# Weight conversions of a mixed attention and MLP kernel: low parts made by TensorE in place of GpSimd, and copies moved to ScalarE

## The chip, the cores and the metric

The kernel runs on one core of a Trainium2 chip. The metric is the device time of one execution in microseconds, as the median of several runs. The engines are named as the profile names them: PE (TensorE matmul), PEld (its weight loads), DVE (VectorE), ACT (ScalarE), POOL (GpSimd) and SP (SyncE, which issues most DMAs).

## The reference

Three parts follow one another, for 4 batches, 768 tokens and 384 channels (8 heads of 48).

```python
# 1: delta-rule attention, per head, k normalized
for t in range(S):
    y[:, :, t] = q_t @ state
    state = state + beta_t * outer(k_t, v_t - state.T @ k_t)
# 2: Fourier mixing and MLP
u = x + real(fft(fft(x, axis=1), axis=2))
x = u + relu(layernorm(u) @ w_ch1) @ w_ch2          # 384 -> 1536 -> 384
# 3: token mixing
theta = x @ w_theta
u = x + w_tok_r @ (x * cos(theta)) + w_tok_i @ (x * sin(theta))
out = u + relu(u @ w_ch)
```

The weights `w_ch1`, `w_ch2`, `w_theta`, `w_tok_r`, `w_tok_i` and `w_ch` are multiplied in two parts each: a high one in the rounded format fp32r and a low one that holds the rest, with three matmuls for one product (`mm3`). They arrive as 64-bit floats.

## The kernel before

The work is written as one Python program whose instructions a scheduler of the framework orders on each engine, by the order of the program and a simulated timeline. Each engine then runs its own list in order. `tc.issue_after(ins)` puts what is traced inside it behind `ins` on that instruction's engine.

**Attention.** Tokens are taken in 48 scans of one batch and 64 tokens each (8 heads, as 4 pairs). Two scans make a chunk step d (24 of them), four chunk steps a wave w (6). For each wave `gram` loads keys (`kt`) and forms products of keys with keys and queries, which ACT copies to `KQ` (L220) and POOL completes with copies of a diagonal block (L223). `solve` inverts 128 triangular 32x32 systems on DVE: a transpose (L228), a few small instructions with a square root on ACT (L240), then 60 dependent multiplications and additions in a loop (L258, L261). `solved` transposes the result. `chunks(d)` makes from it the operands `YU` of two scans: copies by DVE (L309, L315), matmuls, copies by ACT. `load(d)` fetches queries and keys, `scan(g)` runs the recurrence: matmuls on PE with copies by ACT (L340 and others) between them. The generator `attention_steps` writes these steps out in order, with `SOLVES` and `GRAMS` saying at which chunk step a later wave is solved or formed. `attend(n)` advances it by n yields.

**Weight conversion.** `Split.steps` takes one 128x384 block of a 64-bit weight at a time: SP loads it (`raw`), ACT takes the absolute value of the upper words (L110), DVE assembles the 32-bit float and the rest in six instructions (L111 to L116, on the tiles `a` and `g` that the profile calls `w_0ag`, `w_384ag` and so on by the block's first column), and POOL makes the high part (L120), the difference (L121) and the low part (L122). `w1` and `w2` have 24 blocks together. Twenty are written between the attention steps of batch 0, behind the end of solve 0 on DVE, the others before the first MLP matmul.

**Fourier and MLP.** After the 12 scans of a batch `fourier_inputs` forms sums on DVE and POOL (L395), `fourier_1` and `prepare_1` multiply by constants, normalize (L530 and after) and `prepare_2` transposes. Twelve MLP blocks q (three a batch, 256 tokens each) follow, each with twelve steps f of `ffn_up` (9 matmuls into `ph`, L72 to L74) and `ffn_down` (6 into `pc`, L595 to L598). The preparation of block q+1 is written at f = 0, 4 and 11 of block q (`LEAD`). After each step the attention of the next batches advances by `attend(PACE)`, later the conversion of the token-mixing weights.

**Token mixing.** Phases (`pth`) and products (`ty`, `tc`) follow at the end.

Four PSUM buffers with the tags `g` (three) and `mw` (one) serve nearly all of this until the last part.

Of the kernel before, what the change touches and what calls it, by code (L numbers as in the profile page):

```python
# [33 lines left out]
F64_LEAST = 2.0 ** -15  # L34
F64_MOST = float(np.array([0x47EFFE00], np.uint32).view(np.float32)[0])
# [6 lines left out]
SOLVES = (2, 6, 7, 13, 15)  # L42
GRAMS = (1, 6, 9, 13)
CONV_AT = 0
CONV_PRE = 9
# [7 lines left out]
AHEAD = {3: (), 4: (5,), 5: (6, 7)}  # L53
FIXD = ()
SUBD = 0
# [5 lines left out]
CONV_0 = 1  # L61
FDVE = 2
EVERY = 1
PACE = 2
# [12 lines left out]
class Split:  # L77
# [15 lines left out]
    def steps(self, stage, act=False):  # L93

        nc, step = self.nc, self.STEP
        for c, s in self.todo:
# [40 lines left out]
class Front:  # L137
# [19 lines left out]
    def open_attention(self, ctx):  # L157
# [13 lines left out]
        self.Y3 = [win.tile([P, 2, 8, D], F32, name=f"Y3{i}") for i in range(NY3)]  # L171
        self.beta = self.sml.tile([P, NW, 32], F32, name="beta")
# [28 lines left out]
    def gram(self, w, c0=0, c1=2 * C):  # L201

        nc, FE, TK, B2 = self.nc, self.FE, self.TK, self.B2
        if c0 == 0:
            self.KQ[w] = self.sol.tile([P, NI, 2 * C], F32, tag="KQ", name=f"KQ{w}", bufs=2)
# [3 lines left out]
        for d in range(4 * w, 4 * w + 4):  # L209
            for h in range(0, 8, step):  # L210
                n = slice(8 * (d % 4) + h, 8 * (d % 4) + h + step)
                kt = self.sol.tile([P, step, 8 * C // step], F32, tag="kt", name=f"kt{d}_{h}_{c0}", bufs=NKT)
                for par in range(2):
                    nc.sync.dma_start(kt[FE[par]], src[par, d, :, h:h + step])
                sm = self.mw([P, step, c1 - c0], f"sm{d}_{h}_{c0}")
                for i in range(step):
                    for par in range(2):
                        k = kt[FE[par], i, :]
                        self.mm(sm[TK[par], i, :], k[:, 0:C], k[:, c0:c1])
                nc.scalar.activation(kq[:, n, c0:c1], sm, AF.Copy)  # L220
                if c0 == 0:
                    for par in range(2):
                        (nc.vector if w in FIXD else nc.gpsimd).tensor_copy(kq[B2[par], n, 0:32], kq[B2[par], n, 32:64])  # L223

    def solve(self, w):
        nc, sol, sml = self.nc, self.sol, self.sml
        T = sol.tile([P, 32, 32], F32, tag="T", name=f"T{w}")
        nc.vector.transpose(T.rearrange("p j i -> p j i"), self.KQ[w][:, :, 0:32].rearrange("p n j -> p j n"))  # L228
        diag = T.rearrange("p i j -> p (i j)")[:, 0:1024:33]

        def small(nm, bufs=1):
            return sml.tile([P, 32], F32, tag=nm, name=f"{nm}_{w}", bufs=bufs)

        s0, rc, nr, g, ng = (small(nm) for nm in ("s0", "rc", "nr", "g", "ng"))
        nT = small("nT", 2)
        dg = small("dg")
        nc.vector.tensor_copy(dg, diag)
        nc.gpsimd.affine_select(out=T, in_=T, compare_op=ALU.is_gt, fill=0.0, base=0,
                                pattern=[[1, 32], [-1, 32]], channel_multiplier=0)
# [12 lines left out]
        nc.vector.tensor_tensor(T, T, ng.unsqueeze(2).to_broadcast([P, 32, 32]), ALU.mult)  # L252
        nc.vector.memset(diag, 1.0)
        tmp = sml.tile([P, 256], F32, tag="tmp", name=f"tmp{w}")
        for j in range(1, 31):
            n = 31 - j
# [772 lines left out]
```

## Time and profile before

| | us |
|---|---|
| time, median of 3 runs (lowest to highest) | 1001.59 (1001.2 to 1005.55) |
| profiled execution, span from first to last instruction | 1217.0 |
| PE busy in the span | 1126.0 (93%) |
| DVE busy | 682.7 (56%) |
| ACT busy | 394.8 (32%) |
| POOL busy | 387.5 (32%) |
| mean granted TensorE clock in the profiled execution | 0.666 |

The profiled execution is a single one. Its span is longer than the time of the three runs, and no other time of this execution is recorded. Busy times are unions: matmuls that overlap are counted once. The granted clock is a share of 2.4 GHz.

### The profile page before, as it was taken

How to read it: one execution, taken by the hardware profiler on the slowest of the kernel's cores; microseconds unless marked ns; L12 is line 12 of the kernel's file. 1: busy time of each engine (PE TensorE's matmuls, PEld its weight loads, DVE VectorE, ACT ScalarE, POOL GpSimd, SP SyncE). 2: the span in 40 equal slices, each digit the busy share in tenths (PEclk: the TensorE clock that was granted, in tenths of full speed). 3: DMA queues.
4: the chain of work that ended last, by engine and by line, in shares of the span. 5: the costliest groups of instructions: out<-in, count | busy, mean ns of one | idle time of the engine just before them, and what ended most of it. 6: DMA issues, size and time to landing. Idle time of an engine off the chain costs nothing.

```text
span 1217.0 us, 23437 instructions
## 1 busy us (share of the span) xinstructions
PE 1126.0 (93%) x9312; PEld 957.3 (79%) x9312; DVE 682.7 (56%) x1574; ACT 394.8 (32%) x982; POOL 387.5 (32%) x504
## 2 busy tenths in 40 slices
PE   5675664999999999999999999999999999999998
PEld 4564553778788888788888898888988888888887
DVE  5999999645666632576212464744579732450401
ACT  2243343423332343244352121212545411460300
POOL 5257764341131113024120242430235421350210
PEclk9995555666666666666666666666666666666666
DMA  6223431221030021012030021311132201110000
GB/s 190 70 87 94 121 110 50 79 72 60 29 110 21 28 86 59 27 40 68 27 106 14 26 78 40 91 40 32 47 104 65 85 14 35 38 40 20 20 13 26
DMA packets 42206, 71.87 MB, mean 59 GB/s; under 512 B 6833, under 2 KB 27057, under 8 KB 42097
## 3 DMA queue, kind: packets, MB, share of 16 engines
q1 hardware_dynamic: 41328, 68.02, 18.7%
q0 software_dynamic: 768, 2.36, 0.7%
q8 instruction: 73, 1.20, 0.4%
q14 instruction: 37, 0.30, 0.1%
HBM read 56.20 MB, written 14.16 MB: 58 GB/s over the span
## 4 chain that ended last, share of the span: by engine, by line
PE 83%; DVE 13%; issue 1%; DMA 1%; ACT 1%; POOL 0%; SPq 0%; ACTq 0%; DVEq 0%; POOLq 0%
PE pc L595 6%; PE ph L72 6%; PE ph L74 6%; PE ph L73 6%; PE pc L598 6%; PE pc L596 6%; PE ty L73 6%; PE ty L72 6%; PE ty L74 6%; PE sm L199 3%; PE pm L530 3%; DVE tmp L258 3%; DVE T L261 3%; PE py L199 2%; PE pg L457 2%; PE pu L199 2%
## 5 line engine op out<-in xcount | busy, mean ns | idle before, releaser
L586 DVE SCALAR_TENSOR_TENSOR hl<-ph,hh 128x256 fp32r<-128x256 f32 x144 | 60.1, 421 | 196.6 <-ACT hh L585 164.1
L72 PE MATMUL ph<-uh,w1h 128*128 128x256 f32 x432 | 151.9, 355 | 0.0
L74 PE MATMUL ph<-uh,w1l 128*128 128x256 f32 x432 | 148.5, 345 | 0.0
L73 PE MATMUL ph<-ul,w1h 128*128 128x256 f32 x432 | 148.2, 344 | 0.0
L595 PE MATMUL pc<-w2h,hh 128*128 128x384 f32 x288 | 127.6, 443 | 0.0
L585 ACT ACTIVATE hh<-ph 128x256 fp32r<-128x256 f32 x144 | 54.5, 383 | 208.6 <-PE ph L74 183.0
L596 PE MATMUL pc<-w2l,hh 128*128 128x384 f32 x288 | 121.4, 422 | 0.0
L199 PE MATMUL sm<-kt 48*64 48x128 f32 (+1 forms) x896 | 87.5, 354 | 30.7 <-DMA kt<-in_kq_dram 17.3
L73 PEld LDWEIGHTS ph<-ul,w1h 128*128 128x128 f32 x432 | 100.7, 233 | 6.6 <-issue 2.2
L72 PEld LDWEIGHTS ph<-uh,w1h 128*128 128x128 f32 x432 | 97.4, 226 | 8.3 <-issue 2.5
L74 PEld LDWEIGHTS ph<-uh,w1l 128*128 128x128 f32 x432 | 101.0, 234 | 2.3 <-issue 0.8
L199 PEld LDWEIGHTS sm<-kt 48*64 48x64 f32 x896 | 67.5, 186 | 43.7 <-ACT KQ L220 12.5
L598 PE MATMUL pc<-w2h,hl 128*128 128x384 f32 x288 | 98.2, 425 | 0.0
L261 DVE TENSOR_TENSOR T<-T,tmp 128x30 f32<-128x30 f32 (+9 forms) x180 | 73.1, 406 | 4.2
L258 DVE TENSOR_TENSOR tmp<-T 128x30 f32<-128x30 f32 (+9 forms) x180 | 72.9, 405 | 4.3
L284 POOL TENSOR_SCALAR_AFFINE_SELECT YQ<-KQ 64x512 f32<-64x512 f32 x48 | 33.1, 690 | 131.5 <-PE py L199 122.8
L199 PE MATMUL py<-X,YQ 112*64 112x48 f32 (+1 forms) x768 | 54.4, 259 | 22.3 <-ACT X L340 22.1
L595 PEld LDWEIGHTS pc<-w2h,hh 128*128 128x128 f32 x288 | 63.3, 220 | 8.4 <-issue 4.0
L596 PEld LDWEIGHTS pc<-w2l,hh 128*128 128x128 f32 x288 | 63.2, 220 | 7.2 <-issue 1.7
L199 PE MATMUL pu<-X,YU 128*64 128x48 f32 (+1 forms) x768 | 46.2, 262 | 23.6 <-ACT X L352 11.7
L199 PEld LDWEIGHTS py<-X,YQ 112*64 112x64 f32 (+1 forms) x768 | 45.3, 184 | 28.7 <-ACT X L340 23.9
L199 PEld LDWEIGHTS pu<-X,YU 128*64 128x64 f32 (+1 forms) x768 | 38.7, 181 | 33.9 <-ACT X L352 12.2
(282 smaller groups left out, 2524.6 us busy)
## 6 DMA issues: line engine op xcount, KB each, us to landing
kt<-in_kq_dram SPq DMA_DIRECT2D x96, 96.0 KB, 2.2
w_0raw<-in_w_dram SPq DMA_DIRECT2D x15, 384.0 KB, 3.4
YQ<-in_qt_dram SPq DMA_DIRECT2D x48, 96.0 KB, 2.4
Y<-in_kn_dram SPq DMA_DIRECT2D x48, 96.0 KB, 2.4
X<-in_v_dram SPq DMA_DIRECT2D x48, 96.0 KB, 2.5
ysc<-y SPq DMA_DIRECT2D x24, 192.0 KB, 2.1
x2scr<-u SPq DMA_DIRECT2D x12, 384.0 KB, 2.8
xt<-x2scr SPq DMA_DIRECT2D x24, 192.0 KB, 2.4
```

The source lines that it names most:

```text
L72: nc.tensor.matmul(out, lh, rh, start=start, stop=False)
L73: nc.tensor.matmul(out, lh, rl, start=False, stop=False)
L74: nc.tensor.matmul(out, ll, rh, start=False, stop=stop)
L199: self.nc.tensor.matmul(o, l, r, start=True, stop=True, skip_group_check=True)
L258: nc.vector.tensor_tensor(pr, T[:, j + 1:, j:j + 1].to_broadcast([P, n, j]), T[:, j, 0:j].unsqueeze(1).to_broadcast([P, n, j]), ALU.mult)
L261: nc.vector.tensor_tensor(T[:, j + 1:, 0:j], T[:, j + 1:, 0:j], pr, ALU.add)
L530: nc.tensor.matmul(pm, G[:, ch, j * P:(j + 1) * P], cs2[:, ch, :], start=(ch == 0), stop=(ch == KD - 1))
L585: nc.scalar.activation(hh, ph, AF.Relu)
L586: self.up_end = nc.vector.scalar_tensor_tensor(hl, ph, 0.0, hh, ALU.max, ALU.subtract)
L595: nc.tensor.matmul(self.pc[i], hh[:, i * P:(i + 1) * P], wh, start=(f == 0), stop=False)
L596: nc.tensor.matmul(self.pc[i], hh[:, i * P:(i + 1) * P], wl, start=False, stop=False)
L598: nc.tensor.matmul(self.pc[i], hl[:, i * P:(i + 1) * P], wh, start=False, stop=(f == KF - 1))
```

## The change

- In `steps`, w1 and w2 get a new way to make the two parts (`sums`): ACT copies the high part `oh`; the low words times their scale, negated, go to `ol`; PE adds `af - ol - oh` in one PSUM tile with an identity and a negated identity as weights; ACT copies the sum to `ol`. POOL takes no part. The assembly of the float needs one DVE instruction less, since the scale 2^-80 is put into ACT's absolute value. The later weights keep POOL's way.
- `gram` loads both key halves with one DMA of 112 partitions (zeros between them); wave 0's third and fourth key tiles use buffers of the MLP. For waves 0 and 1 ACT copies the Gram diagonal from PSUM (`DIAG_ACT`).
- The two kinds of YU copies in `chunks` go to ACT for d = 0 to 5 (`COPY_ACT`).
- A square root on a one-element tile is put at the start (`warm`).
- The order of the attention steps is written out in `PLAN`: k, q, g form Gram products of a chunk step; s solves, j transposes the solution (`solved`); l, c, n are load, chunks and scan; f loads the Fourier constants; w and W write conversions, W behind the end of the solve written last; a bar ends one `attend`.
- Conversions that the plan doesn't hold (18 to 24) are written when block 0 needs them, at the latest at f = 5; the preparation of block 1 is written at f = 5, 7 and 11. `attend` advances once a step.
- A two-block form of the solve with a `join` is added; with `BLOCKED = 0` it doesn't run.

```diff
+F64_SCALE = 2.0 ** -80
-SOLVES = (2, 6, 7, 13, 15)
-GRAMS = (1, 6, 9, 13)
-CONV_PRE = 9
+BLOCKED = 0
+COPY_ACT = (0, 1, 2, 3, 4, 5)
+DIAG_ACT = (0, 1)
+LEAD_0 = (5, 7, 11)
+PLAN = """k0 k1 k2 k3 w1 s0 q0 q1 q2 q3 l0 l1 g4 g5 g6 g7 j0 c0 c1 f n0 W1 n1 W1 l2 c2 W1 n2
+ W1 n3 W1 l3 c3 W1 g8 g9 g10 g11 W1 s1 W1 n4 W1 n5 W1 l4 j1 c4 W1 n6 W1 n7 W1 l5 n8 W1
+ n9 W1 l6 c5 n10 W1 n11 l7 c6 c7 s2 n12 | n13 l8 j2 c8 g12 g13 g14 g15 | s3 n14 | n15 l9 c9
...
-PACE = 2
 # Split.steps
-            nc.scalar.activation(af, high.bitcast(F32), AF.Abs)
-            nc.vector.tensor_scalar(g, high, 0x80000000, None, ALU.bitwise_and)
+            nc.scalar.activation(af, high.bitcast(F32), AF.Abs, scale=F64_SCALE)
+            nc.vector.tensor_scalar(g, high, 0x80000000, 0x80000000, ALU.bitwise_xor, ALU.bitwise_and)
             nc.vector.tensor_scalar(af, af, F64_LEAST, F64_MOST, ALU.max, ALU.min)
-            nc.vector.tensor_scalar(a, a, 3, 0x40000000, ALU.logical_shift_left, ALU.bitwise_xor)
-            nc.vector.scalar_tensor_tensor(a, a, 0x7FFFFFFF, g, ALU.bitwise_and, ALU.bitwise_or)
+            nc.vector.scalar_tensor_tensor(a, a, 3, g, ALU.logical_shift_left, ALU.bitwise_xor)
             nc.vector.tensor_scalar(g, a, 0xFF800000, None, ALU.bitwise_and)
+            if sums:
+                ps, eye, minus = sums(f"{self.name}_{c}_{s}s")
+                nc.vector.scalar_tensor_tensor(ol, low, -(2.0 ** -52), gf, ALU.mult, ALU.mult)
+                nc.scalar.activation(oh, af, AF.Copy)
+                nc.tensor.matmul(ps, eye, af, start=True, stop=False)
+                nc.tensor.matmul(ps, minus, ol, start=False, stop=False)
+                nc.tensor.matmul(ps, minus, oh, start=False, stop=True)
+                nc.scalar.activation(ol, ps, AF.Copy)
+                yield
+                continue
 # Front.init
+        s = self.sml.tile([P, 1], F32, name="warm")
+        nc.gpsimd.memset(s, 1.0)
+        nc.scalar.activation(s, s, AF.Sqrt)
 # Front.gram, for one chunk step d
+            if c1 == C and d % 4 >= NKT:
+                kt = self.up.tile([P, 2, DM], F32, tag=("u", "u", "un")[d % 4 - NKT], ...)
...
-                for par in range(2):
-                    nc.sync.dma_start(kt[FE[par]], src[par, d, :, h:h + step])
+            nc.sync.dma_start(kt[0:P - 16], src[d, :, h:h + step])
...
+            if w in DIAG_ACT:
+                nc.scalar.activation(kq[:, n, c0:c1], sm, AF.Copy)
+                for par in range(2):
+                    nc.scalar.activation(kq[B2[par], n, 0:32], sm[B2[par], :, 32:C], AF.Copy)
+                continue
 # Front.copy, new, called in chunks in place of nc.vector.tensor_copy
+        if d in COPY_ACT:
+            self.nc.scalar.activation(o, i, AF.Copy)
+        else:
+            self.nc.vector.tensor_copy(o, i)
+    def sums(self, name):
+        return self.psg.tile([P, DM], F32, tag="g", name=name), self.ident, self.eyes
 # attention_steps, "W"
+                with self.tc.issue_after(self.solve_end.ins):
+                    for _ in range(n):
+                        self.convert()
 # front, block 0
+    def converted(n):
+        while fr.done < n:
+            fr.convert()
...
+    converted(3)
     h = fr.ffn_up(*blocks[0], 0, *ready[0])
     for n, (q, f) in enumerate(order):
-        for _ in range(3 if q == 0 else 0):
-            next(split, None)
+        lead = LEAD if q else LEAD_0
+        if f in lead and more:
+            if q == 0:
+                converted(24)
+            prep(q + 1, lead.index(f))
...
+            if q1 == 0:
+                converted(6 * (f1 // 3) + 3)
             nh = fr.ffn_up(*blocks[q1], f1, *ready[q1])
+        if q == 0:
+            converted(6 * (f // 3) + 4 + f % 3)
```

## Rows read from the trace of the kernel before

**Rows 1.** Five stretches: busy us (instructions) of each engine, granted clock, DMA share, GB/s.
```profile
0.00:29.20 29.20, 15.88 (x224) 14.23 (x224) 16.30 (x36) 8.72 (x16) 15.06 (x36) 1.00 0.69 190
29.20:53.20 24.00, 18.84 (x160) 16.16 (x160) 21.89 (x62) 5.03 (x10) 7.45 (x17) 1.00 0.30 86
53.20:190.00 136.80, 81.58 (x1362) 70.98 (x1360) 133.20 (x266) 53.04 (x134) 93.51 (x98) 0.65 0.34 101
190.00:234.00 44.00, 32.19 (x472) 26.06 (x473) 37.65 (x96) 16.93 (x49) 9.64 (x21) 0.58 0.13 39
234.00:1217.00 983.00, 977.50 (x7100) 829.91 (x7096) 473.66 (x1117) 311.03 (x775) 261.86 (x334) 0.65 0.17 50
```

**Rows 2.** Chain that ended last, 0 to 60 us: start, length, what.
```profile
6.49 3.54 DMA kt<-in_kt_dram
...
22.45 1.28 ACT L240
```

**Rows 3.** Timeline of DVE, 15 to 30 us; in brackets idle before and releaser.
```profile
17.11 1.90 DVE L228 STREAM_TRANSPOSE T<-KQ 128x1024 f32<-128x1024 f32 x1 [5.24 <-POOL KQ L223]
...
24.01 0.18 DVE L241 TENSOR_SCALAR s<-s 128x32 f32<-128x32 f32 x1 [4.77 <-ACT s L240]
...
29.25 0.66 DVE L258 TENSOR_TENSOR tmp<-T 128x30 f32<-128x30 f32 x1
```

**Rows 4.** Groups by line, DVE, 53.2 to 190: busy us, mean ns | idle before.
```profile
L261 DVE TENSOR_TENSOR T<-T,tmp 128x30 f32<-128x30 f32 (+14 forms) x41 | 24.2, 590 | 0.5
L258 DVE TENSOR_TENSOR tmp<-T 128x30 f32<-128x30 f32 (+14 forms) x41 | 23.5, 573 | 0.5
L116 DVE SCALAR_TENSOR_TENSOR w_0ag<-w_0raw,w_0ag 128x384 f32<-128x384 uint32 x11 | 8.2, 762 | 0.0
L309 DVE COPY YU<-TT 32x256 f32<-32x256 f32 x16 | 6.6, 411 | 0.5
L315 DVE COPY YU<-TT 32x256 f32<-32x256 f32 x16 | 5.9, 369 | 0.5
...
L113 DVE TENSOR_SCALAR w_0ag<-w_0ag 128x384 uint32<-128x384 uint32 x11 | 3.9, 372 | 0.0
...
L116 DVE SCALAR_TENSOR_TENSOR w_1152ag<-w_1152raw,w_1152ag 128x384 f32<-128x384 uint32 x2 | 1.1, 540 | 0.0
```

**Rows 5.** Groups by line, DVE, 289.9 to 333.8 us (solve 3).
```profile
L261 DVE TENSOR_TENSOR T<-T,tmp 128x30 f32<-128x30 f32 (+14 forms) x30 | 9.9, 331 | 0.8
L258 DVE TENSOR_TENSOR tmp<-T 128x30 f32<-128x30 f32 (+14 forms) x30 | 9.8, 328 | 0.8
```

**Rows 6.** POOL busy with lines L120, L121 and L122, in this order.
```profile
53.20:190.00 136.80, 23.92 (x19) 0.65 0.34 101
...
53.20:190.00 136.80, 24.10 (x19) 0.65 0.34 101
...
53.20:190.00 136.80, 21.69 (x19) 0.65 0.34 101
```

**Rows 7.** Groups by line, ACT, 0 to 225 us.
```profile
L316 ACT ACTIVATE YU<-pt 32x256 f32<-32x256 f32 x18 | 6.7, 373 | 1.1 <-PE pt L199 0.7
L110 ACT ACTIVATE w_0ag<-w_0raw 128x384 f32<-128x384 f32 x12 | 6.5, 552 | 30.4 <-DMA w_0raw<-in_w_dram 29.9 <-POOL w1l L122 0.4
L340 ACT ACTIVATE X<-pu 64x192 f32<-64x192 f32 x15 | 4.9, 324 | 4.8 <-PE pu L199 4.5
```

**Rows 8.** Chain that ended last, 130 to 240 us.
```profile
185.51 1.00 DVE y L395
...
234.07 0.32 PE ph L72
```

**Rows 9.** Timeline of PE, about 250 and 1042 us: start, length, what.
```profile
250.16 2.17 PE L530 MATMUL pm<-cs,G 128*128 128x385 f32 x4
...
1042.16 0.40 PE L74 MATMUL pth<-wthh,xl 128*128 128x384 f32 x1
1042.39 0.40 PE L72 MATMUL pth<-wthh,xh 128*128 128x384 f32 x1
```

More of the change, by code (lines that the diff above doesn't have):

```diff
@@ L225, in solve @@
+            nc.scalar.activation(kq[:, n, c0:c1], sm, AF.Copy)
+            for par in range(2):
+                nc.gpsimd.tensor_copy(kq[B2[par], n, 0:32], kq[B2[par], n, 32:C])
     def solve(self, w):
         nc, sol, sml = self.nc, self.sol, self.sml
-        T = sol.tile([P, 32, 32], F32, tag="T", name=f"T{w}")
+        nb = 2 if w < BLOCKED else 1
+        m = 32 // nb
+        buf = sol.tile([P, 33 * 32], F32, tag="T", name=f"T{w}")
+        T = buf[:, 0:1024].rearrange("p (i j) -> p i j", j=32)
@@ L308, in chunks @@
         for par in range(2):
[L309 removed]
+            self.copy(d, yu[B2[par], par, :, 32:64], TT[B2[par], n, :])
         pt = self.mw([P, 8, 32], f"pt{d}")
@@ L641, in front @@
     fr.init()
-    steps = fr.attention_steps()
-    state = {"chunks": 0, "fed": 0}
+    steps = fr.attention_steps(PLAN)
+    state = {"fed": 0}
+    fr.scans = 0
     back = []
@@ L651, in attend @@
                 return
-            g = state["chunks"]
+            g = fr.scans
             if g // 2 % 6 >= 2 and fr.stage1 < g // NCH - 1:
@@ L658, in attend @@
                 return
-            s = next(steps, None)
-            if s is not None:
-                state["chunks"] = s
+            next(steps, None)
             feed()
@@ L665, in feed @@
         b = state["fed"]
-        if state["chunks"] >= NCH * (b + 1) and fr.stage1 >= b - 1:
+        if fr.scans >= NCH * (b + 1) and fr.stage1 >= b - 1:
             with tc.high_priority(offset=FOFF):
@@ L669, in feed @@
             state["fed"] = b + 1
-    attend(1)
-    a, c = fr.w1.steps(fr.stage, SUBD), fr.w2.steps(fr.stage, SUBD)
-    def splits():
-        for _ in range(4):
-            for _ in range(3):
-                next(a)
-                yield
-            for _ in range(3):
-                next(c)
-                yield
-    split = splits()
-    for _ in range(CONV_0):
-        next(split)
-    attend(1)
-    fr.load_fourier()
-    late = None
+    a, c = fr.w1.steps(fr.stage, 0, fr.sums), fr.w2.steps(fr.stage, 0, fr.sums)
+    fr.split = chain.from_iterable(zip(range(k, k + 3), x) for k in range(1, 24, 6) for k, x in ((k, a), (k + 3, c)))
+    fr.done = 0
+    def converted(n):
+        while fr.done < n:
+            fr.convert()
     while not state["fed"]:
         attend(1)
-        if state["chunks"] >= CONV_AT:
-            late = late or fr.solve_end
-            with tc.issue_after(late.ins):
-                next(split, None)
     fr.early = False
@@ L716, in front @@
         prep(0, part)
-    for _ in range(CONV_PRE):
-        next(split, None)
     order = [(q, f) for q in range(len(blocks)) for f in range(KF)]
+    converted(3)
     h = fr.ffn_up(*blocks[0], 0, *ready[0])
@@ L722, in front @@
         more = q + 1 < len(blocks)
-        for _ in range(3 if q == 0 else 0):
-            next(split, None)
-        if f in LEAD and more:
-            prep(q + 1, LEAD.index(f))
+        lead = LEAD if q else LEAD_0
[3 more added lines that the diff above has]
+            prep(q + 1, lead.index(f))
         nh = None
```

184 lines of the change are left out of this document (116 added, 68 removed).

## The prediction

> **What bounds the kernel now.** I read the busy time by stretches first, then the chain of waits, then the groups by line inside the stretches that these two point to. The stretches [rows 1] split the span at 234 us, where the first MLP matmul runs [rows 8]. Behind it lie 983 us in which PE is busy for 977.5: PE's own work is the bound there, at a granted clock of 0.65, between its two levels of 1.2 and 2.4 GHz. Ahead of it lies a head in which PE is busy for only 148.5 of 234 us. From 53.2 to 190 us DVE is busy for 133.2 of 136.8 us and the chain of waits runs along DVE; POOL has 93.5 us there, PE 81.6, ACT 53.0. So the head ends when DVE has done its work, and everything after it is PE.
>
> DVE's work in the head is not what it would be alone. The solve loop (L258, L261) has the same 60 small instructions in every wave. In solve 3, where POOL does little, they take 328 and 331 ns [rows 5]; in the 53.2 to 190 stretch 573 and 590 ns [rows 4]. L116 takes 762 ns beside POOL's work and 540 ns in the two conversions that were not disturbed [rows 4]. POOL's own busiest lines there are the three conversion instructions, 23.9 + 24.1 + 21.7 = 69.7 us, 75% of its 93.5 [rows 1, 6].
>
> How the profile stands to the median: the profiled span is 1217.0 us, the median of three runs 1001.6. DVE, ACT and POOL set the head in both; the difference fits PE running slower in the profiled execution. If all of it lies behind 234 us, the timed run needs (1001.6 - 234) / 983 = 0.78 of the profiled time there (what lies around the span is not recorded; it would make this slightly smaller). I make the sum against the profiled span and multiply what falls behind 234 us by 0.78.
>
> **The change part by part.**
>
> *Start of the first solve.* The key loads of chunks 2 and 3 wait for a free `kt` buffer: issue at 6.49, 3.54 us to landing [rows 2]. With two more buffers they need not wait; about 3.5 us. The Gram diagonal is copied by ACT straight from PSUM, so DVE's transpose at 17.11, which waited 5.24 us for POOL's copies [rows 3], follows the last Gram copy. DVE then waits 4.77 us for the square root [rows 3], of which the table load on ACT is 1.28 [rows 2]; the new `warm` line takes that load to the start. Least: 3.5 + 1.3 = 4.8 us. Most: 3.5 + 5.2 + 1.3 = 10. I take 8, because the two waits of the middle overlap in part. The Trainium skill (ScalarE: Activation LUTs, What ACT_TABLE_LOAD costs) gives about 2.7 us for a table load; by it this edit would give 1.4 us more, but the row of this trace says 1.28.
>
> *Conversions lose their POOL work.* Each of the 19 conversions in the stretch has three POOL instructions, all gone. What DVE gains is the stretching they cause. The 82 loop instructions take 23.5 + 24.2 = 47.7 us instead of 82 x 0.33 = 27.1: 20.6 us; L116 adds up to 19 x 0.22 = 4.2. POOL's conversions are 75% of what stretched them: 18.5 us. Below, counting the loop alone, 15; above, if all 133.2 us of DVE were stretched as L116 is, 133.2 x (1 - 540 / 762) x 0.75 = 29. I take 22, nearer the lower end, since no clean value is shown for the rest.
>
> *DVE work removed or moved.* L113 (372 ns [rows 4]) is folded into L114's instruction: 17 conversions x 0.37 = 6 us. The YU copies of chunks 0 to 5 go to ACT: 12 x 411 + 12 x 369 ns = 9 us [rows 4]. The plan has 17 conversions in the head where 20 were: six DVE lines each, from L113's 0.37 to L116's 0.76 us, some 2.7 together: 3 x 2.7 = 8 us later.
>
> *What ACT and PE take over.* ACT gets two 384-column copies for each conversion, about 0.55 us each as L110 [rows 7], 24 YU copies of 0.37 us as L316 [rows 7], and 24 small diagonal copies of at most 0.37: 19 + 9 + 9 = 37 us, covered by ACT's idle time (53.0 busy of 136.8). PE gets three 384-column matmuls a conversion. By start-to-start times an fp32r one costs 0.23 us (1042.16 to 1042.39) and an fp32 one 0.47 (four in 2.17, the last running out) [rows 9]: 0.47 + 2 x 0.23 = 0.93 us. In the head that is 16 us, at 1.2 GHz 0.65 / 0.5 as long, 21 us, covered by PE's 55 idle us of the stretch; without that cover it would be a loss of as much. The 7 conversions that are left until after the first MLP matmul have no cover: 7 x 0.93 = 6.5 us. The Trainium skill (FP8 and Floating Point Precision, TensorE Precision Notes) gives true fp32 four passes; by it the first matmul would cost 0.92 us and the seven conversions 9.7 us, 3 us more. The rows here show two times an fp32r matmul, so I keep 6.5.
>
> *Padded loads and the written order.* One 112-partition load takes the place of two 48-partition ones, 52 SP issues fewer; SP is not on the chain after the start, so nothing. The plan names the same steps in nearly the same order as the generator it replaces. The scale by a power of two adds no instruction; `BLOCKED` is 0, so `join` never runs.
>
> *What is late next.* The shorter head leaves less idle PE time. By 225 us fifteen scans and nine chunks had been evacuated [rows 7], three of each more than the twelve scans and six chunks that the first block needs; some of that will now fall into the PE stretch. PE's 32.2 us between 190 and 234 [rows 1] hold them beside the Fourier and preparation work; I put them at no more than a third, 11 us, and let 6 return. Conversions 18 to 24 and the block's `u` share two buffers, so they follow each other, a load and then 2.7 us of DVE each; the matmuls of f = 9 to 11 stand behind them on PE in order. For that wait I take 3 us; 10 is the worst.
>
> *Sum.* Head: 8 + 22 + 6 + 9 + 8 = 53 us of DVE. Not all of it shortens the head: from 185.51, where the Fourier sums begin [rows 8], to 234 the path alternates between DVE, PE and ACT. I count 45. Behind: 6.5 + 6 + 3 = 15.5 us of PE, times 0.78 = 12. Profiled span at equal clock: 1217 - 45 + 15.5 = 1187. Median: 1001.6 - 45 + 12 = 968.6; I say 968.
>
> **The rivals.** *The gain is kept in part.* PE and ACT take their instructions in order. A conversion's second and third matmul wait for DVE and ACT, and ACT's low copy waits for PE; chunks and scans queued behind them wait too. Against it: PE is idle 40% of the stretch, and the solves, which hold DVE, need no scan. For it: before, conversions touched PE not at all, so this coupling is new. If 10 to 16 conversions each hold the scans for 1.5 us, the head shrinks by 20 to 30 instead of 45: 984 to 994.
>
> *The gain is larger.* If POOL's stretching lay on all DVE work (29 us) and the scans, freed of POOL's queue, keep up, the head shrinks by 60 and the PE stretch pays 8: 950 or less, down to 940.
>
> *Slower.* The coupling in full: a conversion holds the scan path for the rest of its DVE work (a line like L113 and L116, 0.37 + 0.76), its matmuls (1.2 at 1.2 GHz) and the ACT copy (0.55), 2.9 us. Sixteen of them are 46 us, the whole head gain, and the 12 us of PE work stand alone: 1014. It decides from (45 - 12) / 16 = 2.1 us for each conversion; at that point nothing changes. Against it: scans 0 to 7 need only solve 0 and have the length of solve 1 to run in.
>
> *No change.* DVE is not the bound that it looks like, and the head's end stays with the scans: 997 to 1006.
>
> **How the numbers follow.** Forecast (head 35 to 53, 957 to 981): 0.57. Kept in part (981 to 997): 0.20. Larger (938 to 957): 0.12. Within 0.5% (about what a measurement of this kernel can tell from no change): 0.04. Slower: 0.07. So faster 0.89, same 0.04, slower 0.07. The range 943 to 995 leaves out a part of the larger case, the end of the partial one and all above it, less than 2 in 10.
>
> **What would show it.** Right: no POOL instruction of w1 and w2 conversions; the loop of solves 1 and 2 near 350 to 400 ns; the first solve starting near 21 us; the first MLP matmul near 190 us; PE still full behind it. Wrong: the loop still above 500 ns (then X, YQ and the select on POOL do the stretching); PE or ACT waiting on conversion tiles in the head with scans behind; gaps in PE within the first MLP block; or a different granted clock behind the head, which would move the time without any step of mine.

## The result, and the profile after

The changed kernel takes 990.67 us in the median of four runs (987.38 to 998.51), the kernel before beside it 1001.88: a ratio of 0.9895, 95% interval [0.9851, 0.9938]. That is 11 us faster where I had forecast 33.6. Eight later runs of the same kernel (e16_after_again below) have a median of 994.95, all twelve 993.2, so the gain is 8 to 11 us. The sign is right, the range holds the time, and it lies in the rival "kept in part" (981 to 997, chance 0.20), not in the forecast.

The profiled execution of before ran PE at 0.65 of its clock all through the MLP blocks [rows 1]; the profiled execution of the changed kernel at 0.97 behind its first MLP matmul. So the kernel before was profiled once more (e0_before below, 1001.87 us), and the other kernels are compared with its stretches. Windows by engine of that profile, columns as in [rows 1]. They run from the start of the span to the loop of solve 0, over that loop, from there to about where the Fourier sums begin (190 us), to the first MLP matmul, and over the rest:

```profile
0.00:27.80 27.80, 14.22 (x195) 12.52 (x195) 15.12 (x36) 7.95 (x14) 12.59 (x33) 1.00 0.72 196
27.80:53.30 25.50, 19.98 (x185) 17.46 (x187) 23.44 (x61) 5.75 (x12) 8.77 (x18) 1.00 0.28 81
53.30:190.00 136.70, 82.85 (x1371) 72.08 (x1367) 133.15 (x267) 53.21 (x135) 94.04 (x100) 0.66 0.34 99
190.00:230.80 40.80, 28.13 (x472) 23.39 (x472) 37.10 (x96) 16.50 (x48) 10.23 (x21) 0.75 0.17 50
230.80:1000.20 769.40, 736.40 (x7100) 680.97 (x7096) 485.96 (x1119) 306.97 (x776) 265.04 (x334) 0.99 0.22 63
```

The same view of the changed kernel (span 996.8, the longest of its four runs); the third row ends where the first Fourier product runs:

```profile
0.00:28.40 28.40, 13.94 (x212) 11.64 (x212) 17.27 (x35) 11.24 (x25) 9.78 (x27) 0.74 0.70 208
28.40:51.80 23.40, 18.83 (x176) 15.58 (x176) 21.30 (x61) 9.09 (x24) 1.96 (x3) 0.50 0.33 106
51.80:178.60 126.80, 90.30 (x1588) 71.09 (x1584) 104.06 (x257) 82.23 (x205) 29.44 (x45) 0.74 0.35 105
178.60:205.10 26.50, 26.48 (x288) 20.64 (x288) 16.47 (x45) 10.03 (x32) 3.84 (x12) 0.57 0.11 32
205.10:996.80 791.70, 757.86 (x7152) 696.30 (x7148) 480.28 (x1100) 319.25 (x795) 252.06 (x324) 0.97 0.21 64
```

Three things are to be seen. The first solve starts no earlier (28.4, before 27.8). The first MLP matmul comes at 205.1 instead of 230.8, 26 us earlier, where 45 had been counted. And the rest takes 791.7 instead of 769.4, 22 us more, where 12 had been counted. In the head DVE is no longer full: it is busy for 104 of 126.8 us.

The rest can be split at the last matmul into `ph`, where the twelve MLP blocks end. From the first to the last `ph` matmul the kernel before needs 508.4 us and the changed kernel 522.8, 14 more. What follows, token mixing for the most part, takes longer too (e0_before, the changed kernel, e16):

```profile
739.30:1000.20 260.90, 239.73 (x1336) 231.92 (x1334) 145.06 (x262) 100.51 (x214) 99.41 (x99) 0.98 0.18 53
```
```profile
727.90:996.80 268.90, 245.31 (x1341) 236.24 (x1339) 142.86 (x248) 101.56 (x214) 98.34 (x100) 0.96 0.16 51
```
```profile
721.50:987.90 266.40, 241.99 (x1341) 232.39 (x1339) 143.79 (x248) 101.54 (x214) 99.65 (x100) 0.98 0.17 52
```

In all eighteen profiles with the new assembly of the floats (the changed kernel and the others below) this last part takes 266 to 270 us, also without the sums on PE (e3_pool_parts, e10_no_sums) and with the old written order (e8_before_pe). For the kernel before there is one profile at this clock, and no run tests the assembly alone, so the cause is not shown.

The relief of DVE did happen. Groups by line, DVE, changed kernel, 51.8 to 178.6 us (L301 and L304 are L258 and L261 of [rows 4]):

```profile
L301 DVE TENSOR_TENSOR tmp<-T 128x58 f32<-128x58 f32 (+14 forms) x59 | 23.6, 400 | 1.4
L304 DVE TENSOR_TENSOR T<-T,tmp 128x84 f32<-128x84 f32 (+14 forms) x58 | 21.7, 374 | 1.4
```

They took 573 and 590 ns and now take 400 and 374. In e0_before the loop of solve 1 has 45.0 us of GpSimd work in it and takes 56.3 us; in the changed kernel 3.2 and 27.3. Instructions that no GpSimd work overlaps take 324 and 323 ns there.

**The start.** The chain of the changed kernel, and below it ACT's and DVE's timelines:

```profile
11.46 0.60 SPq L376
12.10 0.59 SPq L376
12.79 3.61 DMA w_0raw<-in_w_dram
```
```profile
16.43 0.56 ACT L115 ACTIVATE w_0ag<-w_0raw 128x384 f32<-128x384 f32 x1 [4.83 <-DMA w_0raw<-in_w_dram]
17.01 0.60 ACT L247 ACTIVATE KQ<-sm 128x512 f32<-128x512 f32 x1
```
```profile
18.43 1.94 DVE L264 STREAM_TRANSPOSE T<-KQ 128x1024 f32<-128x1024 f32 x1
...
28.45 0.66 DVE L301 TENSOR_TENSOR tmp<-T 128x30 f32<-128x30 f32 x1
```

The third and fourth key tile now hold both `u` buffers. The first conversion, which the plan writes ahead of solve 0, loads into such a buffer, so its load is issued at 12.79 us, behind ten other loads that SP issues from 6.23 us on. ACT's Abs for it (L115) stands ahead of the last Gram copy (L247), and the transpose behind that copy runs at 18.43, where it ran at 17.11 [rows 3].

### The profile page after: what moved, and what is told of

Same layout as the page of the kernel before. It is cut to its first block, busy times and chain, and to the rows that moved or that the text cites. A ratio compares the mean times of both kernels' runs of the same rounds, so it can differ in the third digit from the quotient of the medians.

```text
span 996.8 us, 23415 instructions
## 1 busy us (share of the span) xinstructions
PE 907.4 (91%) x9408; PEld 815.3 (82%) x9408; DVE 639.4 (64%) x1496; ACT 431.8 (43%) x1078; POOL 297.1 (30%) x410
## 4 chain that ended last, share of the span: by engine, by line
PE 56%; DVE 26%; DMA 6%; ACT 5%; issue 4%; POOL 2%; SPq 1%; DVEq 0%; ACTq 0%; POOLq 0%
PE ty L79 4%; PE ty L78 4%; PE ty L77 4%; PE ph L77 4%; PE pc L676 4%; PE ph L78 4%; PE ph L79 4%; DVE tmp L301 4%; PE pc L679 3%; PE pc L677 3%; DVE T L304 3%; PE sm L218 3%; PE pg L535 2%; PE pm L611 2%; PE py L218 2%
## 5 line engine op out<-in xcount | busy, mean ns | idle before, releaser
L77 PE MATMUL ph<-uh,w1h 128*128 128x256 f32 x432 | 125.9, 295 | 1.7 <-DVE ul L655 1.3
L78 PE MATMUL ph<-ul,w1h 128*128 128x256 f32 x432 | 123.9, 287 | 0.7 <-DVE ul L655 0.5
L79 PE MATMUL ph<-uh,w1l 128*128 128x256 f32 x432 | 122.8, 285 | 0.0
L676 PE MATMUL pc<-w2h,hh 128*128 128x384 f32 x288 | 104.2, 362 | 2.6 <-ACT hh L666 2.6
L677 PE MATMUL pc<-w2l,hh 128*128 128x384 f32 x288 | 97.3, 338 | 0.0
L77 PEld LDWEIGHTS ph<-uh,w1h 128*128 128x128 f32 x432 | 81.5, 190 | 5.0 <-DVE ul L655 1.7
L679 PE MATMUL pc<-w2h,hl 128*128 128x384 f32 x288 | 76.9, 345 | 0.7 <-DVE hl L667 0.7
L301 DVE TENSOR_TENSOR tmp<-T 128x30 f32<-128x30 f32 (+9 forms) x180 | 67.5, 375 | 4.7
L304 DVE TENSOR_TENSOR T<-T,tmp 128x30 f32<-128x30 f32 (+9 forms) x180 | 65.1, 362 | 4.9
L377 POOL TENSOR_TENSOR X<-X,nT 64x384 f32<-64x384 f32 x48 | 42.6, 887 | 58.0 <-DMA X<-in_v_dram 47.1
L218 PE MATMUL py<-X,YQ 128*64 128x48 f32 (+1 forms) x768 | 45.6, 235 | 7.4 <-ACT X L418 7.3
L679 PEld LDWEIGHTS pc<-w2h,hl 128*128 128x128 f32 x288 | 49.8, 188 | 1.8 <-DVE hl L667 1.1
L218 PEld LDWEIGHTS py<-X,YQ 128*64 128x64 f32 (+1 forms) x768 | 36.3, 148 | 16.3 <-ACT X L418 8.2
```

Of the source, the lines that this page charges most:

```text
L77: nc.tensor.matmul(out, lh, rh, start=start, stop=False)
L78: nc.tensor.matmul(out, lh, rl, start=False, stop=False)
L79: nc.tensor.matmul(out, ll, rh, start=False, stop=stop)
L218: self.nc.tensor.matmul(o, l, r, start=True, stop=True, skip_group_check=True)
L301: nc.vector.tensor_tensor(pr, E[:, :, j + 1:, j:j + 1].to_broadcast([P, nb, n, j]), E[:, :, j, 0:j].unsqueeze(2).to_broadcast([P, nb, n, j ...
L304: nc.vector.tensor_tensor(E[:, :, j + 1:, 0:j], E[:, :, j + 1:, 0:j], pr, ALU.add)
```

## The experiments

Beside each group of kernels the kernel before was run again. Its medians are 1002.82 us beside e0, e2, e6 and e3, 1002.38 beside e8, e7, e1 and e4, 1002.31 beside e9 to e12, 1002.51 beside e13 to e16, and 1002.42 beside e17 and e18. A ratio is a kernel's time by that of before, with its 95% interval.

**Profile again, and where the late conversions stand** (e0_before, e2_all_before, e6_24_in_plan, e3_pool_parts).

> The kernel before, unchanged, for a profile at a granted clock that can be compared with the one of the changed kernel. Both theories: first MLP matmul near 234 us as in the first profile, since the head is not PE's; if the slow PE of the first profile is all that set the 1217 us apart, PE's stretch shrinks to some 765 us. Theory A (the gain of the head is given back in block 0): here block 0 runs without a hole, its twelve steps in 55 to 65 us. Rival B (nothing is given back, PE's stretch is as long in both): the changed kernel's stretch behind the first MLP matmul (792 us) is no longer than the one of this kernel by more than 5 us.

```diff
 # e2_all_before: all 24 before the first MLP matmul, block 1 prepared as before
-    converted(3)
+    converted(24)
-        lead = LEAD if q else LEAD_0
+        lead = LEAD
 # e6_24_in_plan: at seven places n4 to n9
-W1
+W2
 # e3_pool_parts: low and high parts by GpSimd again
-    a, c = fr.w1.steps(fr.stage, 0, fr.sums), fr.w2.steps(fr.stage, 0, fr.sums)
+    a, c = fr.w1.steps(fr.stage, 0), fr.w2.steps(fr.stage, 0)
```

> All 24 conversions are written before the first MLP matmul, and the preparation of block 1 again at f = 0, 4 and 11. Theory A (seven late conversions, which follow each other through one raw buffer, hold block 0 from 220 to 256 us): the hole in block 0 goes, the first MLP matmul comes 12 to 25 us later than at 205, and the time stays within 6 us of the changed kernel, since the loads of the conversions are only moved. Rival B (what was lost lies in the coupling of PE, ACT and DVE in the head, not in block 0): 15 to 20 us slower than the changed kernel, the price of seven more conversions in the head.

> Seven more conversions stand in the written order between scans 4 and 10, where DVE was idle for 20 of 80 us; nothing is left for block 0. Theory A: no hole in block 0, the first MLP matmul 5 to 15 us later than at 205, and 5 to 15 us faster than the changed kernel. Rival B: each further conversion holds the scans behind it by 2 to 3 us, the first MLP matmul comes 15 to 20 us later, and the time is the same or slower.

> The changed kernel with the high and low parts of w1 and w2 made by POOL as before; DVE keeps its shorter assembly, all else is unchanged. Theory A with contention as predicted: the loop of solves 1 and 2 goes from about 350 and 410 ns an instruction back to 480 to 560, the first MLP matmul comes 15 to 25 us later, and the time is 10 to 20 us above the changed kernel. Rival B (DVE's stretching did not set the head's end, the scans did): the loop is as slow, but the time is within 4 us of the changed kernel.

Measured: e0 1001.87; e2 1001.97, ratio 0.9982 [0.9959, 1.0004]; e6 1003.02, 0.9988 [0.9971, 1.0006]; e3 1022.01, 1.0185 [1.0151, 1.0218]. In e0 block 0 runs without a hole, in 45.4 us, less than the 55 to 65 of Theory A. Seven more conversions ahead of the first MLP matmul move it to 243.8 (e2) and 227.2 us (e6) and cost the whole gain. So leaving them for block 0 is worth 9 to 12 us. With GpSimd's parts the same plan is some 30 us slower than with TensorE's, more than the 10 to 20 of Theory A: the plan depends on the sums.

**Single parts** (e8_before_pe, e7_raw_in_un, e1_first_late, e4_yu_on_dve).

```diff
 # e8_before_pe: the kernel before, with the new assembly and the sums on PE only
-    a, c = fr.w1.steps(fr.stage, SUBD), fr.w2.steps(fr.stage, SUBD)
+    a, c = fr.w1.steps(fr.stage, SUBD, fr.sums), fr.w2.steps(fr.stage, SUBD, fr.sums)
 # e7_raw_in_un: conversions 18, 20, 22, 24 load into another buffer
+        if self.staged >= 17 and self.staged % 2:
+            raw = self.up.tile([P, 2, DM], F32, tag="un", name=name + "raw", bufs=1)
 # e1_first_late: first conversion behind solve 0
-PLAN = """k0 k1 k2 k3 w1 s0 ... n0 W1 n1
+PLAN = """k0 k1 k2 k3 s0 ... n0 W2 n1
 # e4_yu_on_dve
-COPY_ACT = (0, 1, 2, 3, 4, 5)
+COPY_ACT = ()
```

> The kernel before with one part of the change alone: the low parts by PE and the shorter assembly; order, loads and copies as before, all conversions ahead of the first MLP matmul. Theory A (POOL's stretching of DVE was the price in the head): the loop of solves 1 and 2 falls from 613 and some 500 ns to 350 to 420, the first MLP matmul comes 10 to 25 us before 231, and the time is 980 to 992. Rival B (a conversion on PE and ACT holds the scans as long as POOL held DVE): first MLP matmul within 6 us of 231, time 997 to 1005.

> The changed kernel; the raw words of every second late conversion (18, 20, 22, 24) go to the buffer of the normalized input, so two loads can be in flight. Theory A (the late conversions follow each other through one buffer, 7 us each, and hold block 0, where PE also drops to its half clock): block 0 shrinks from 84 to 55 to 70 us and the time falls by 5 to 13 us. Rival B (the hole costs nothing, since PE does later attention in it): block 0 shorter, block 5 starts at 480 as before, time within 3 us of the changed kernel.

> The changed kernel with its first conversion moved from ahead of solve 0 to behind scan 0, so that ACT does not wait for its load ahead of the last Gram copy. Both: the first transpose on DVE at about 12 in place of 18.4 us, solve 0's loop from 23 to 25 in place of 28.4. Theory A (the chain through solve 0 still sets the head): first MLP matmul and time 3 to 5 us earlier. Rival B (behind solve 0 loads, PE and ACT set the head): first MLP matmul within 2 us of 205 or later, time within 3 us.

> The changed kernel with the YU copies of chunk steps 0 to 5 on DVE again. Theory A (DVE sets the head): 9 us of DVE come back, 5 to 9 us slower. Rival B (DVE has 20 idle us between 52 and 130 in the changed kernel, and ACT holds the scans): within 2 us, or faster.

Measured: e8 997.92, 0.9944 [0.9915, 0.9972]; e7 991.0, 0.989 [0.9825, 0.9955]; e1 990.59, 0.9876 [0.9845, 0.9907]; e4 994.28, 0.9912 [0.9888, 0.9937]. The sums alone (with the new assembly) bring less than half of the gain. In e8 the first Fourier product comes at 189.7 (210.1 in e0_before), but the first MLP matmul at 235.7 (230.8), as its Rival B had it: the last four conversions come in between, one after the other (their first matmuls run from 211.1 to 235.1). The last `ph` matmul is 10.7 us earlier than in e0_before, and the last part takes 7 of that back. e7 shortens the wait of f = 6 (below) from 38 to 22 us and block 0 from 84 to 61 us, and the time by nothing.

e1 starts solve 0 at 26.6 us, 1.8 earlier, and nothing of it reaches the end. It is no clean test of the start, because the same load still stands ahead of solve 0, now ahead of the square root on ACT instead of the last Gram copy (its chain):

```profile
14.57 5.70 DMA w_0raw<-in_w_dram
...
20.29 0.54 ACT w_0ag L115
20.84 0.13 ACT s L283
```

e4 is 1 us above the median of all twelve runs of the changed kernel, which can't be told from nothing.

**Is the head set by DVE's chain, or by the sums on PE?** (e9 to e12)

```diff
 # e9_late_and_un: e1 and e7 together
 # e10_no_sums
-                nc.tensor.matmul(ps, eye, af, start=True, stop=False)
-                nc.tensor.matmul(ps, minus, ol, start=False, stop=False)
-                nc.tensor.matmul(ps, minus, oh, start=False, stop=True)
-                nc.scalar.activation(ol, ps, AF.Copy)
 # e11_late_pool: conversions 18 to 24 take the other way (high part on ACT, rest on GpSimd)
     def sums(self, name):
+        if self.staged > 17:
+            return None
 # e12_head_delay: in solve(w), ahead of the loop
+        for _ in range(10 if w == 1 else 0):
+            nc.vector.tensor_scalar(buf[:, 0:1024], buf[:, 0:1024], 1.0, None, ALU.mult)
```

> The changed kernel with both earlier edits together: the first conversion behind solve 0, and the raw loads of conversions 18, 20, 22, 24 in the buffer un. Alone the first had its first MLP matmul at 199.5 us (205.1 without) and the time 990.6, the second its sixth MLP block at 474.2 us (480.1 without) and the time 991.0. Theory H (what the head loses the end loses, one for one): both add up, sixth block near 468, time 978 to 984. Theory P (PE's own work sets the time; a shorter head only moves PE's idle time to another place): 987 to 991, and PE's idle time over the whole span stays at 90 to 100 us.

> The changed kernel without the three matmuls and ScalarE's low copy of each conversion; the low part is then the scaled low word alone, so this part of the computation is left out. In the changed kernel these matmuls have 2.4 us of PE records for each conversion (41 us before the first MLP matmul, 17 behind it), where I had counted 0.93. Theory S (this price, and what is queued behind it, is what ate the gain): behind the first MLP matmul alone 17 us less, in the head up to 15: 960 to 974. Theory P with the sums hidden in PE's idle time: only the start-to-start time of the seven late ones, 7 x 0.93 = 6.5 us: 983 to 986. If the head's end hangs on DVE and scans alone: first MLP matmul still at 200 to 206 us.

> The changed kernel, with conversions 18 to 24 alone made without TensorE: ScalarE copies the high part, GpSimd subtracts and adds the low word, as before. The other 17 stay on PE. Theory S: the late sums cost PE 17 us that nothing covers, so 974 to 984, and PE's busy time from the first MLP matmul to the sixth block falls by 15 or more. Rival (the late conversions are paced by their loads and buffers, and PE does attention in between): time 988 to 993, and the first block still takes 80 us or more.

> The changed kernel with ten more DVE instructions of 128x1024 (a multiplication by 1.0 of the solve's own matrix, some 1.1 us each) ahead of the loop of solve 1: 11 us more on the chain that leads to the head's end, and no PE work added. Theory H: first MLP matmul at 216, time 1001 to 1002. Theory P (PE's work sets the time, and in the 11 us PE can do scans and Gram products that it would do later): 991 to 996.

Measured: e9 989.93, 0.9876 [0.9848, 0.9904]; e10 993.45, 0.991 [0.9883, 0.9937]; e11 983.46, 0.9799 [0.9765, 0.9834]; e12 983.38, 0.9815 [0.9787, 0.9842].

e9 lies in Theory P's range: both edits together bring nothing that can be told, and PE's idle time over the span is 93 us.

e12 falls outside both theories. DVE's timeline shows the delay where it was put (the first three and the last four of the ten added instructions, then the loop; the lines left out hold the other three and a conversion):

```profile
72.59 2.15 DVE L298 TENSOR_SCALAR T<-T 128x1024 f32<-128x1024 f32 x3
...
78.20 2.87 DVE L298 TENSOR_SCALAR T<-T 128x1024 f32<-128x1024 f32 x4
...
81.53 0.20 DVE L303 TENSOR_TENSOR tmp<-T 128x30 f32<-128x30 f32 x1
```

Solve 1's loop runs from 81.5 to 108.7 instead of 71.8 to 99.1. The first Fourier product still comes at 176.8 (178.6 without), the first MLP matmul at 196.4, and the kernel is faster. So a DVE chain that is 9.6 us longer at solve 1 moves the head's end by nothing here, and Theory H is out. The time is taken up between solves 1 and 2, where DVE has idle time. Behind that DVE is full again in the changed kernel, up to the first Fourier product:

```profile
140.10:178.60 38.50, 24.84 (x572) 19.51 (x567) 36.27 (x95) 23.48 (x62) 9.94 (x13) 0.86 0.31 94
```

Of these 36.27 us some 24 are the loop of solve 2, which batch 0 does not need. From 168 us to that product PE is busy for 1.09 of 10.6 us and waits for the Fourier sums, which share DVE with that loop. So e12 does not show that the head's end is free of DVE altogether. Why e12 is faster than the changed kernel is not settled: the scheduler gave every engine a somewhat different order.

e10 is out the other way. Without the sums scan 7 comes later (142.0, with them 133.8), the last scan of batch 0 at about the same time (162.4, with them 160.8), and PE is idle for 81.5 of the head's 212 us, with them for 55.5 of 205. So it is not shown that the sums in the head ate the gain, as Theory S had it. The first Fourier product comes 30.2 us behind the last scan, with the sums 17.8. In that time DVE is full and PE waits (e10, the last 22.6 us before the product):

```profile
170.00:180.00 10.00, 0.14 (x6) 0.01 (x2) 9.25 (x28) 0.00 (x0) 1.55 (x2) 0.64 0.23 75
180.00:192.60 12.60, 4.95 (x108) 4.47 (x108) 12.34 (x23) 5.00 (x15) 1.47 (x2) 0.50 0.06 17
```

For the late ones the time of Theory S holds: e11 against the changed kernel, and e15 against e9 below, are each worth about 1% (10 us). From the first to the last `ph` matmul e10 takes 511.9 us and e11 511.6, the changed kernel 522.8.

**The wait of f = 6.** PE's timeline in the changed kernel, one late conversion, the first matmul of the next and the first of f = 6; the lines left out are attention:

```profile
248.90 1.65 PE L124 MATMUL w_0s<-w_0ag,ident 128*128 128x384 f32 x2 [0.77 <-DVE w_0ag L118]
249.88 0.98 PE L125 MATMUL w_0s<-w2l,eyes 128*128 128x384 f32 x1
250.67 0.52 PE L126 MATMUL w_0s<-w2h,eyes 128*128 128x384 f32 x1
...
255.21 1.65 PE L124 MATMUL w_0s<-w_0ag,ident 128*128 128x384 f32 x2
256.09 0.99 PE L77 MATMUL ph<-uh,w1h 128*128 128x256 f32 x1
```

The matmuls of f = 5 began at 218.3, those of f = 6 at 256.1. They need none of conversions 18 to 24. They stand behind them in PE's order, because `converted(24)` is written at f = 5, and the conversions come one by one as their loads land (ACT waits up to 3.5 us for one, DVE up to 4.8). PE fills the hole with attention. Windows of the hole, and of the stretch of e11 from f = 5 on, where the same conversions go past PE and f = 6 follows after 4.1 us:

```profile
218.50:256.00 37.50, 33.12 (x388) 24.73 (x387) 19.39 (x55) 18.82 (x44) 7.56 (x15) 0.68 0.33 103
```
```profile
221.30:240.00 18.70, 18.70 (x223) 15.00 (x221) 8.78 (x23) 9.11 (x22) 9.96 (x15) 1.00 0.40 119
```

PE counts as busy in most of both, but in the hole at 0.68 of its clock. How much of the 10 us is the wait and how much the sums' own PE time, no run separates; e7, with 16 us less of the wait, needs 518.9 us for the blocks instead of 522.8.

**The clock, the order, and a faster version** (e13 to e18).

```diff
 # e13_warm_fourier (behind the last scan of batch 0), e14_warm_start (behind the products of k3)
+    def warm(self, n, name):
+        t = self.psg.tile([P, P], F32, tag="g", name=name)
+        for _ in range(n):
+            with self.tc.issue_after(self.last.ins):
+                self.mm(t, self.eyes, self.eyes)
 # e15_three: e1, e7 and e11 together;  e16_after_again: the changed kernel
 # e17_lead_later: on the changed kernel;  e18_four: on e15_three
-LEAD_0 = (5, 7, 11)
+LEAD_0 = (8, 10, 11)
```

> The changed kernel with 40 small matmuls of constants (128x128, not part of the computation) on PE behind the last scan of batch 0, where PE is idle in the changed kernel from 168 to 180 us and then runs at half clock until 201, through the Fourier products and the preparation of the first block. Theory C (what the shorter head gained was in part given back by PE's granted clock, 147 us at half clock against 117 before): the clock stays at 1.00 there, the first MLP matmul comes near 196 instead of 205, the half-clock time falls by 20 to 30 us and the time to 980 to 985. Rival (the order of the instructions, not the clock): the clock changes and the time stays at 988 to 993, or the added matmuls delay the Fourier products and it is 995.

> The changed kernel with the same 40 matmuls behind the four Gram products of the start, where PE is idle from 12 to 18 us in the changed kernel and at half clock from 15 to 75. Theory C: with the clock kept, up to 60 us less at half clock; but PE mostly waits for DVE in that stretch, so little of it shows: solve 1 at 70 to 72 as before, time 985 to 991. If PE's latency matters for the chunks and scans there, 980 to 985. Rival: the clock falls anyway a few us later, nothing changes, 989 to 993.

> The changed kernel with three edits that each stood alone: first conversion behind solve 0, raw loads of 18, 20, 22, 24 in the buffer un, and conversions 18 to 24 made without TensorE. Theory C with S: late sums off PE were worth 7 us alone (983.5), the other two nothing that could be measured alone; together 978 to 984. If a run with less PE work in the late conversions loses the clock there again: 985 to 990.

> The changed kernel unchanged, once more, for a second profile beside the others on one chip: the first profile was the slowest of its four runs (998.5, granted clock 0.913; the others 0.922 to 0.931). Time 988 to 993. Theory C: if this profile has a higher clock, its head's instructions come in the same order, and the difference to the first profile lies in stretches where one has half clock and the other not.

> The changed kernel with the preparation of block 1, and with it the writing of conversions 18 to 24 ahead of everything else, at f = 8, 10, 11 of block 0 in place of 5, 7, 11. In the changed kernel the matmuls of f = 6 wait 35 to 38 us for these conversions, and PE does attention in between, at half clock. Theory L (this wait is where the gain was given back: attention that fills a hole alone costs PE twice what it costs between MLP matmuls): the wait at f = 6 falls under 10 us and is spread over f = 6 to 9, block 0 takes 55 to 70 us, time 980 to 987. Rival (the conversions' own pace, a pair every 7 us, sets the block; the wait moves to f = 9 whole, or block 1 waits for its preparation): the first three blocks take the 182 us that they take now, 988 to 995.

> The kernel with three edits (first conversion behind solve 0, raw loads of 18, 20, 22, 24 in un, late conversions without TensorE), which took 980.1, and the preparation of block 1 written at f = 8, 10, 11 as well. Theory L: its wait at f = 6 is 11 us; without it 973 to 979. Rival: nothing left to gain there, or block 1 waits for its preparation: 979 to 984.

Measured: e13 1003.58, 1.0009 [0.9991, 1.0026]; e14 1003.9, 1.0018 [0.9998, 1.0038]; e15 980.14, 0.9772 [0.974, 0.9804]; e16 994.95 in eight runs, 0.9927 [0.9898, 0.9955]; e17 1004.54, 1.0001 [0.9971, 1.0031]; e18 980.19, 0.9747 [0.9702, 0.9791].

e16 is the changed kernel, instruction for instruction. Windows of four us around its Fourier products, first the earlier profile, then e16:

```profile
168.00:172.00 4.00, 0.00 (x0) 0.00 (x0) 3.83 (x10) 0.00 (x0) 2.19 (x2) 0.86 0.54 167
...
180.00:184.00 4.00, 4.00 (x25) 3.37 (x24) 3.86 (x9) 0.00 (x0) 0.41 (x4) 0.50 0.00 0
184.00:188.00 4.00, 4.00 (x25) 3.48 (x23) 3.84 (x7) 0.99 (x2) 0.23 (x2) 0.50 0.00 0
...
196.00:200.00 4.00, 4.00 (x86) 3.53 (x87) 2.33 (x7) 2.38 (x7) 0.82 (x1) 0.50 0.22 70
```
```profile
168.00:172.00 4.00, 0.76 (x28) 0.61 (x22) 3.83 (x10) 0.00 (x0) 2.19 (x3) 1.00 0.39 102
...
180.00:184.00 4.00, 4.00 (x32) 3.55 (x31) 3.86 (x11) 0.20 (x2) 0.41 (x4) 0.72 0.02 4
184.00:188.00 4.00, 4.00 (x46) 2.94 (x44) 3.90 (x5) 1.91 (x5) 0.44 (x4) 1.00 0.00 0
```

PE idles for DVE's Fourier sums in both, and drops to half clock (1.2 GHz) in both. In e16 it is back at 2.4 GHz at 182 us, in the other only at 201. The first MLP matmul follows at 198.7 and at 205.1. The two spans, 987.9 and 996.8, differ by 9 us: 6.4 of them are here, the other 2.6 in the last part, where the slower one has 0.96 of the clock and the other 0.98. Over the twelve runs of this kernel the time goes with the time at half clock (twice the missing share of the mean clock, times the span): 136 us and 987.4 at one end, 182 and 999.0 at the other, slope 0.26, correlation 0.92.

e13 and e14 did not do what they were meant to. e13's 40 matmuls took 4.7 us and were over when the idle time began:

```profile
164.00:168.00 4.00, 3.24 (x67) 3.00 (x65) 3.73 (x8) 0.00 (x0) 2.75 (x3) 1.00 0.59 142
168.00:172.00 4.00, 0.00 (x0) 0.00 (x0) 3.90 (x12) 0.00 (x0) 0.14 (x1) 0.67 0.35 132
172.00:176.00 4.00, 0.00 (x0) 0.00 (x0) 4.00 (x14) 1.46 (x4) 0.00 (x0) 0.50 0.00 0
```

In e14 the clock fell at 20 us instead of 15 and stayed at half until about 80. Both are some 9 us above e16; in both the wait of f = 6 was 38 to 40 us long. They leave open whether holding the clock would have helped. Against e16, e13 loses most of its time in the MLP blocks (530.0 us, e16 522.9), e14 ahead of the first MLP matmul (210.7, e16 198.7).

e17 answers its question against Theory L: the wait left f = 6 and came whole at f = 9 (230.1 to 269.3, 502 PE instructions at a mean clock of 0.73), since the conversions were now also written later. Block 0 took 90.9 us, with the old lead 81.7 to 84.3. Its rival had named this move of the wait, but for a time of 988 to 995. e18 changes nothing on top of e15 that can be told. e15_three, with a ratio of 0.9772 some 22 us faster than before, and e18 are the fastest of all. In e15 the wait at f = 6 is 11 us, and the MLP blocks take 509.7 us, one more than in the kernel before.

## Why the prediction was wrong, step by step

**Contention: right.** The loop of solves 1 and 2 was to fall from 573 and 590 ns to 350 to 400; it fell to 400 and 374. In the loop of solve 1 of e0_before an instruction takes 613 ns where GpSimd's work overlaps it and 324 where none does. The Trainium skill (SBUF — State Buffer, Who interferes with whom) says that only the port pair that DVE shares with GpSimd causes contention, as an exclusive lock; these 613 and 324 ns are in line with it, though no trace shows the port. From the loop of solve 0 to the end of solve 1 the head became 34 us shorter (104.9 to 70.7).

**Start: failed.** Forecast 8 us, measured -0.6. The two buffers given to the keys were taken from the first conversion's load, and its Abs and its DVE work went ahead of the last Gram copy and of the transpose. I had costed the padded loads and the written order at nothing and did not ask which tile was next to wait for a `u` buffer. e1 moves it and gains 1.8 us, with the load still ahead of solve 0; what a start without it is worth, no run shows.

**Head behind solve 1: failed.** I counted 45 of 53 us of DVE's relief as a shorter head, on the premise that "the head ends when DVE has done its work". From the end of solve 1 to the first Fourier product the changed kernel needs 79.5 us, before 77.4: nothing gained, though DVE has less to do. The stretch between the loops of solve 1 and solve 2, e0_before, then changed kernel:

```profile
132.70:164.00 31.30, 17.25 (x296) 14.88 (x296) 30.65 (x53) 11.62 (x30) 19.76 (x25) 0.50 0.38 115
```
```profile
99.10:140.10 41.00, 33.95 (x460) 26.48 (x456) 25.27 (x53) 26.77 (x67) 14.40 (x27) 0.75 0.45 137
```

DVE is full in the first and has 25 of 41 us in the second. There it waits 9.6 us once for PE's first sum matmul (L124) to free the conversion's tile and 4.9 for a load; the chain runs over a 3.64 us load of keys and ScalarE's Gram and YU copies. e12 agrees: DVE's chain has 10 us to spare there. The scans set no better pace than before up to scan 4: scan 0 at 70.0 (68.7), scan 4 at 100.0 (99.8), and only from there on earlier, the last of batch 0 at 160.8 (183.6). What set their pace is not shown. DVE does wait for PE on a conversion's tile, as the rival "kept in part" had feared of such coupling, but its mechanism, sums that hold the scans, is not shown: in e10, without them, the last scan is no earlier. That the time lies in its range is luck as far as is known.

Behind the first Fourier product the head of the changed kernel loses another 5.8 us (26.5 to the first MLP matmul, before 20.7), at a granted clock of 0.57; e16, at 0.92, loses nothing there (19.5).

**PE stretch: mechanism right for the MLP blocks, the last part missing.** Forecast 12 us at the timed pace, measured 20 (e16) to 22. Of these 14 lie in the MLP blocks, close to the forecast, and 5.5 (e16) to 8 in the last part, where the sum had no term. The wait behind conversions 18 to 24 I put at 3 us, 10 at worst, ahead of f = 9 to 11. It is 35 to 38 us ahead of f = 6, although the change itself said that they are written at the latest at f = 5, and the attention that fills it brings back most. Its net price with the sums is the 10 us of e11, where my two terms (6.5 + 3, times 0.78) have 7.4. The sums themselves were close: at full clock one conversion's three occupy 1.11 us in the trace (222.44 to 223.55) for 0.93 forecast.

**The clock: not in the sum.** I had named a different clock only as something that "would move the time without any step of mine". The change itself moves it: the changed kernel's runs spend 136 to 182 us at half clock, those of before 120 in the median. By the slope of 0.26 the difference of some 30 us would be worth 8. That is an estimate, and one run speaks against carrying the slope from kernel to kernel: e10 spends 178 to 202 us at half clock and takes 993.45. What is shown is that two executions of one kernel differ by 9 us where their clocks differ.

Together, by spans: 33 us were forecast, 45 less 12. In e16 the head is 32 us shorter and the rest 20 longer, which is the 12 us by which its span is below that of e0_before (987.9, 1000.2). In the first profile it is 26 and 22, or 3 us (996.8). The largest miss is the head, 13 to 19 us: more than 8 of them at the start, the rest behind solve 1.

What stays open: why the last part is longer, and why e12, e13 and e14, which alter little, move the time by 10 us and more in either direction. The scheduler reorders every engine's list after each edit, and I have no run that separates order from edit.

## What to carry to other kernels

When an engine at 97% is relieved, look for the chain that is second, stretch by stretch, and test it with a delay: ten idle instructions on the relieved engine show whether there is slack behind that place, and at that place only, as far as the rest keeps its order. A step moved to an engine that works in order has two prices: its own instructions (here seven conversions of 1.11 us at full clock) and what stands behind them until their operands arrive (here a wait of 35 to 38 us, mostly filled with other work). Moving only the late conversions off PE again was worth 10 us for both, nearly as much as the whole change. Compare every stretch of the two kernels, also those that the change does not seem to touch: the last part gave back 5 to 8 us. And a freed buffer or a lent one has a next user: name it before a load is called free.

## What the runs showed of the hardware

Over the twelve runs of the changed kernel each us at half clock goes with 0.26 us of time. In the kernel before it is far less (75 runs at mean clocks of 0.93 to 0.98, slope 0.03, correlation 0.31): in e0_before nearly all of it falls into the head, where PE waits for DVE. The Trainium skill (TensorE: Matmul & The Clock Gate, Terms) puts the penalty at the throttled time times one minus the ratio, which would be half of it here; neither kernel pays that much.

One program in one order came back from half to full clock 19 us apart in two executions (182 and 201 us), and its span differed by 9. A profile is one such draw: the first one of the changed kernel was the slowest of its four runs.
